# Retention in chunks of 64 inside steps of 128, in 64x64 array tiles throughout

## The chip, the core and the metric

One core of a Trainium2 chip runs the kernel. The metric is the time of one execution in microseconds of the device (us), lower is better; the median of several runs is compared. The profile is that of one execution.

## The reference

Two parts follow each other, all in float32. First a retention (attention without softmax, with a decay per head) over 8 batches, 8 heads, 576 positions and head width 64; then a gated MLP whose gate mixes positions.

```python
scores = (1/sqrt(64)) * q @ k.T                        # per batch and head
gamma  = 1 - 2.0 ** (-5 - arange(8))                   # one decay per head
ret    = scores * where(rel >= 0, gamma ** rel, 0)     # rel = row - column
x      = (ret @ v) -> [batch, 576, 512]

h      = max(x @ w_in, 0); u, v = halves of h          # w_in 512 x 1024
v_n    = (v - mean(v)) / sqrt(var(v) + 1e-6)
v_s    = einsum('ts,bsd->btd', w_spatial, v_n) + b_spatial
out    = (u * v_s) @ w_out                             # w_out 512 x 512
```

## The kernel before, in words

**The MLP.** x, the weights and the intermediates are split into a high and a low float32r part, and a product is three matmuls (`mm3`). On PE a batch goes through the stages v (x with the right half of w_in, five position blocks), u (left half, eight tiles), vs (the mixing of positions, eight tiles) and f (w_out, eight tiles). ACT and DVE take the results out of PSUM, split them and build the normalisation of v (statistics, small operations on 128x1, `vn` high and low).

**The retention** works on chunks of C = 128 positions, four per batch, and a tail of TL = 64. The two heads of a pair p lie in the two halves of the 128 partitions. For a chunk, `scores` makes k times q in 64x64 array tiles (the first key half against all 128 queries, the second against its own 64); DVE multiplies by the mask `am` and leaves `at`. `burst(b, c, nx)` issues, in this order on PE: the state update `ds` from k (scaled by POOL with `kd`) and v; the carried part, state `st` times a second copy of q (`qsc`, loaded from `q_x` and scaled by POOL with `qs`); the scores of the next chunk `nx`; and the values, `at` times v, whose second half uses array tiles of 128 rows by 64 columns. Then DVE adds the two halves of `ds` to the state, POOL multiplies the state by `sd`, and `evac` copies the result to x (ACT high part, DVE low part). Two pairs of PSUM banks alternate.

**Order.** Up to the first matmuls of batch 1's own v stage the order on every engine is that of the program: batch 0's retention goes between the splitting of w_in (`front`, `mid`, `back`) and the v blocks of batch 0, and batch 1's retention between the vs and u tiles of batch 0. From there on a scheduler orders the engines: `interleave` runs the retention of batch b+1 (a generator that yields after each burst) beside the stages of batch b. The retention's matmuls keep their program order. All DMAs are issued by SP; `load(b, c)` brings the four parts (q, k, k by position, v) of a chunk, 1 MB, two steps ahead. A recording class issues every operation, so the profile puts them all on one line, L71 (L72 after the change), and groups are told apart by the names of their tiles. In these, r is any PSUM tile of the retention, qkv a chunk's operands, at the masked scores, early, w and f are stages of splitting a weight, raw_v the right half of w_in as loaded, win and wout the split weights, pre two relu'd u tiles, s, mv and sm the statistics of v.

Of the kernel before, what the change touches and what calls it, by code (L numbers as in the profile page):

```python
# [33 lines left out]
def retention_gmlp(ctx, tc, qkv, q_x, qk_t, q_xt, v_t, w_in, w_sp, b_sp, w_out, amask, qscale, kdec, sdec, out):  # L34
# [8 lines left out]
    am = cp.tile([P, 2, NP, C], F32, name="am")  # L43
    qs = cp.tile([P, NP, C], F32, name="qs")
# [8 lines left out]
    st = [cp.tile([P, NP, D], F32, name=f"st{i}") for i in range(3)]  # L53
# [5 lines left out]
    qsc = {}  # L59
    lent = []  # L60
# [36 lines left out]
    banks = [ps_r.tile([P, 2, 512], F32, name=f"r{i}") for i in range(2)]  # L97
    for t in banks:
        ve.memset(t, 0.0)

    def pair():
        banks.reverse()
        return banks[0]
# [3 lines left out]
    def load_qsc(b, c):  # L107
        if (b, c) == (0, NC):
            t = lent[0]
        else:  # L110
            third = (b, c) == (0, 3)
            t = wk.tile([P, NP, C], F32, name=f"qsc_{b}_{c}", tag="vl" if third else "qsc", bufs=1 if third else 2)
        if c < NC:
            dma(t, q_x[b, c - 1].rearrange("p (a n) -> p a n", a=NP))
        else:
            dma(t[:, :, :TL], q_xt[b])
        qsc[b, c] = t

    def load(b, c):
        if b == 0 and c in (2, 3):  # L120
            tag = ("u", "wout0")[c - 2]
            t = cp.tile([P, NDB, S] if c == 2 else [P, NDB, DM], F32, name=f"qkv_{b}_{c}", tag=tag)
            t = t.rearrange("p a n -> p (a n)")
            if c == 2:
                lent.append(t[:, 4 * 512:].rearrange("p (a n) -> p a n", a=NP))
            t = t[:, :4 * 512].rearrange("p (a n) -> p a n", a=4)
# [17 lines left out]
        if c and (b, c) != (0, NC):  # L144
            load_qsc(b, c)
# [28 lines left out]
    dma(qs, qscale)  # L174
# [3 lines left out]
    load_qsc(0, NC)  # L178
# [61 lines left out]
    def mm(out, w, r, start, stop):  # L240
        tc.keep_in_program_order(pe.matmul(out, w, r, start=start, stop=stop))

    at = {}
    half = [slice(i * D, (i + 1) * D) for i in range(2)]

    def rows(c):
        return C if c < NC else TL

    heads = [[(p, i) for p in (2 * j, 2 * j + 1) for i in range(2)] for j in range(NP // 2)]
    heads = heads[0] + heads[1]  # L250

    def side(p, i):
# [24 lines left out]
    def burst(b, c, nx):
        n = rows(c)
        _, _, kn, vv = chunk[b, c]
        ps = pair().rearrange("p i (a n) -> p i a n", a=2)  # L280
        ds = ps[:, :, 0].rearrange("p r (a d) -> p r a d", a=NP)
        o = ps[:, :, 1].rearrange("p j (a n) -> p j a n", a=2)
        if c < NC:
            for p in range(NP):
                for r in range(2):
                    for e in (r, 1 - r):
                        h = 2 * p + side(p, e)
                        hd = slice(h * D, (h + 1) * D)
# [7 lines left out]
        for s in range(n // D):
            for p, i in heads:
                h = 2 * p + i
                e = side(p, i)
                r = half[e] if s == 0 else slice(0, n)  # L300
                t = slice(s * D, (s + 1) * D)
                mm(o[half[i], e, p // 2, t], vv[r, h * D:(h + 1) * D], at[b, c][r, i, p, t], c == 0 and s == 0 and p < 2, s == n // D - 1 and p >= 2)
        if c < NC:
            new, tmp = st[(c + 1) % 2], st[2]
            if c == 0:
                ac.copy(out=tmp, in_=ds[:, 0])
            else:
                ve.tensor_tensor(out=tmp, in0=ds[:, 0], in1=tmp, op=ALU.add)
            ve.tensor_tensor(out=new, in0=ds[:, 1], in1=tmp, op=ALU.add)
            if c + 1 < NC:  # L310
                po.tensor_tensor(out=tmp, in0=new, in1=sd.broadcast_to([P, NP, D]), op=ALU.mult)
        xo[b, c] = o[:, :, :, :n]

    def evac(b, c):
        src = xo[b, c]
        t = slice(c * C, c * C + rows(c))
        hi, lo = ((xs[b][:, i, :, t] if c < NC else xt[:, :, i]).rearrange("p (a j) n -> p j a n", j=2) for i in range(2))
        ac.copy(out=hi, in_=src)
        ve.tensor_tensor(out=lo, in0=src, in1=hi.bitcast(F32), op=ALU.subtract)
        if c == NC:  # L320
            po.tensor_copy(out=xs[b][:, :, :, t], in_=xt.rearrange("p a i n -> p i a n"))

    def retention(b):
        if b not in xs:
            xs[b] = slot(f"x_{b}")
        nxt = [(b, c) for c in range(NC + 1)] + [(b + 1, c) for c in range(2)]
        if (b, 0) not in at:
            prep(b, 0)
            scores(b, 0)
        yield 0.95  # L330
        for c in range(NC + 1):
            nx = nxt[c + 1] if nxt[c + 1][0] < B and (b, c) != (1, NC) else None
# [3 lines left out]
            evac(b, c)  # L336
# [390 lines left out]
```

## Time and profile before

| | |
|---|---|
| runs | 553.85, 554.76, 557.45 us (median 554.76) |
| profiled execution, first to last instruction | 553.7 us |
| instructions | 15312 |
| PE matmuls busy | 536.8 us (97%), 6735 instructions |
| weight loads | 498.0 us (90%) |
| DVE, ACT, POOL busy | 269.0, 207.4, 133.9 us |
| DMA | 64.08 MB |
| mean granted clock of PE | 0.988 |

No time of the profiled execution but its span is given. Busy times of matmuls overlap in parts, and their ends are modelled; starts are what to go by. A group's "idle before" is the time in which its engine stood still ahead of it, with the engine and tile that ended the wait. A chain row is a stretch of the path that ended last. A program matmul of float32 operands stands as two instructions.

### The profile page before, as it was taken

The numbers are of one execution on the slowest core, as the hardware profiler recorded it, in microseconds if no ns is written. First come the engines' busy times: TensorE is split into PE (matmuls) and PEld (weight loads), VectorE is DVE, ScalarE is ACT, GpSimd is POOL, SyncE is SP. The second block draws the span as 40 slices with busy tenths as digits, with TensorE's granted clock in tenths as the row PEclk, the third lists the DMA queues.
The fourth block names the chain that finished last, engine by engine and source line by source line (L and its number), as shares of the span: only waits on it lengthen the run. The fifth ranks groups of instructions, "written<-read, shape, count | busy, mean of one in ns | idle before, by whom it ended". The sixth has DMA issues, their size and how long they took to land.

```text
span 553.7 us, 15312 instructions
## 1 busy us (share of the span) xinstructions
PE 536.8 (97%) x6735; PEld 498.0 (90%) x6735; DVE 269.0 (49%) x588; ACT 207.4 (37%) x447; POOL 133.9 (24%) x133
## 2 busy tenths in 40 slices
PE   6897999899999999999999999999999999999997
PEld 4676998799998899989999899988999899998997
DVE  7685566922643735247351654327353373506240
ACT  4356323742223632236222551226322362226422
POOL 4747557700212111202112120121201122000000
PEclk8898899999999999999999999999999999999999
DMA  8992465002464322533225222342225342020002
GB/s 318 381 310 80 162 193 191 0 22 76 164 180 146 105 80 67 201 118 102 50 96 182 78 96 50 128 150 89 88 55 180 114 149 49 2 76 11 2 1 86
DMA packets 37045, 64.08 MB, mean 116 GB/s; under 512 B 14833, under 2 KB 27249, under 8 KB 33010
## 3 DMA queue, kind: packets, MB, share of 16 engines
q1 hardware_dynamic: 36978, 63.10, 34.5%
q8 instruction: 53, 0.87, 0.7%
q14 instruction: 14, 0.11, 0.1%
HBM read 53.65 MB, written 9.44 MB: 114 GB/s over the span
## 4 chain that ended last, share of the span: by engine, by line
PE 85%; DMA 5%; DVE 5%; ACT 3%; issue 1%; POOL 1%; SPq 0%; ACTq 0%; DVEq 0%
PE vs L71 21%; PE f L71 19%; PE u L71 17%; PE v L71 14%; PE r L71 14%; DMA qkv<-in_qkv 5%; DVE f L71 2%; DVE s L71 1%; ACT x L71 1%; DVE sm L71 1%; ACT vn L71 0%; POOL qsc L71 0%; DVE vn L71 0%; DVE w L71 0%; POOL qkv L71 0%
## 5 line engine op out<-in xcount | busy, mean ns | idle before, releaser
L71 PE MATMUL vs<-wsp,vn 128*128 128x288 f32 x768 | 115.6, 299 | 3.0 <-ACT pre L71 2.4
L71 PEld LDWEIGHTS vs<-wsp,vn 128*128 128x128 f32 x768 | 105.9, 189 | 4.9 <-ACT pre L71 2.7
L71 PE MATMUL u<-x,win 128*128 128x288 f32 x768 | 105.6, 296 | 2.2 <-ACT u L71 2.2
L71 PEld LDWEIGHTS u<-x,win 128*128 128x128 f32 x768 | 103.0, 188 | 3.7 <-POOL f L71 2.5
L71 PE MATMUL v<-win,x 128*128 128x512 f32 x384 | 93.3, 398 | 0.0
L71 PE MATMUL f<-g,wout 128*128 128x288 f32 x672 | 92.3, 296 | 0.0
L71 PEld LDWEIGHTS f<-g,wout 128*128 128x128 f32 x672 | 89.8, 188 | 0.5
L71 DVE TENSOR_TENSOR at<-r,am 128x1024 f32<-128x1024 f32 (+1 forms) x40 | 44.5, 1113 | 94.0 <-PE r L71 94.0
L71 PEld LDWEIGHTS v<-win,x 128*128 128x128 f32 x384 | 71.0, 188 | 16.6
L71 POOL TENSOR_TENSOR qsc<-qsc,qs 128x512 f32<-128x512 f32 (+1 forms) x31 | 36.1, 1165 | 177.5 <-DMA qsc<-in_q_x 112.7
L71 PEld LDWEIGHTS r<-qkv 64*64 64x64 f32 x2176 | 47.3, 139 | 14.0 <-issue 6.6
L71 PE MATMUL r<-qkv 64*64 64x64 f32 (+1 forms) x2176 | 54.0, 240 | 4.6 <-POOL qkv L71 2.8
L71 DVE BATCH_NORM_STATS2 s<-v 128x6 f32<-128x512 f32 (+1 forms) x40 | 27.7, 693 | 60.3 <-ACT v L71 59.3
L71 ACT COPY o<-f 128x288 f32<-128x288 f32 x64 | 25.6, 400 | 72.0 <-PE f L71 71.9
L71 ACT CAST g<-vs 128x288 fp32r<-128x288 f32 x56 | 22.3, 399 | 75.8 <-DVE vs L71 75.8
L71 ACT CAST x<-r 128x512 fp32r<-128x512 f32 x32 | 18.8, 586 | 60.0 <-DVE st L71 60.0
L71 POOL TENSOR_TENSOR qkv<-qkv,kd 128x512 f32<-128x512 f32 x32 | 33.3, 1043 | 32.3 <-DMA qkv<-in_qkv 25.1
L71 DVE TENSOR_TENSOR g<-vs,g 128x288 fp32r<-128x288 f32 x56 | 25.6, 458 | 26.3 <-ACT g L71 26.3
L71 PE MATMUL r<-at,qkv 64*64 64x64 f32 (+1 forms) x1152 | 37.6, 228 | 0.4 <-DVE at L71 0.4
L71 POOL TENSOR_TENSOR st<-st,sd 128x256 f32<-128x256 f32 x24 | 14.9, 620 | 93.4 <-DVE st L71 93.4
L71 DVE TENSOR_TENSOR vs<-vs,u 128x288 f32<-128x288 f32 x56 | 26.0, 464 | 23.0 <-PE vs L71 23.0
L71 PEld LDWEIGHTS r<-at,qkv 64*64 64x64 f32 (+1 forms) x1152 | 32.1, 141 | 2.8 <-DVE at L71 0.6
(73 smaller groups left out, 509.6 us busy)
## 6 DMA issues: line engine op xcount, KB each, us to landing
qkv<-in_qkv SPq DMA_DIRECT2D x31, 1024.0 KB, 5.3
out<-o SPq DMA_DIRECT2D x64, 144.0 KB, 1.8
qsc<-in_q_x SPq DMA_DIRECT2D x24, 256.0 KB, 3.2
raw_v<-in_w_in SPq DMA_DIRECT2D x4, 512.0 KB, 6.5
qkv<-in_qk_t SPq DMA_DIRECT2D x8, 256.0 KB, 3.2
qkv<-in_v_t SPq DMA_DIRECT2D x16, 128.0 KB, 3.4
raw<-in_w_in SPq DMA_DIRECT2D x4, 512.0 KB, 8.4
raw<-in_w_out SPq DMA_DIRECT2D x4, 512.0 KB, 4.1
```

The source lines that it names most:

```text
L71: ins = op(*args, **kw)
```

## The change

A step still takes 128 positions of a batch, but inside it the retention goes by two chunks of 64. Scores are only made within a chunk of 64, so all retention matmuls have 64 rows, 64 columns and a moving part of 64 columns: 272 per batch instead of 240. The state is kept at every 64 positions: `state_half` makes `sh`, the state between the two chunks, and `state_full` the state at the end (`st`); before each addition POOL makes a decayed copy of the other one (`decay`, tiles dec0 and dec1).

POOL scales q in place with `qs` (64 columns, used for both halves); the second copy of q and its loads are gone. The mask now undoes that scaling (it holds gamma to the power of minus the key's position, and zero above the diagonal) and is half as wide. So the scores read q after POOL's multiplication.

The PSUM pair `bo` holds the outputs (o, and ot for the tail), `bs` the scores and the state update; neither alternates. In `burst`, the carried part is issued in two halves, flip 1 (which reads sh for one row half of the array and st for the other) and flip 0, which exchange the row halves and banks. Between them stands `turned`, an ACT copy of two elements into an unused column of bo, which waits for the first half and which the second half waits for. The state update of the next chunk has moved from that chunk's burst into this one, behind its scores. The tail comes from one load, is scored in step 2 of a batch and finished in step 3, so there are four bursts per batch instead of five.

```diff
-    def scores(b, c):
-        n = rows(c)
-        q, k, _, _ = chunk[b, c]
-        ps = pair().rearrange("p i (a n) -> p i a n", a=NP)
-        for s in range(n // D):
-            for p, i in heads:
-                mm(ps[half[s ^ side(p, i)], i, p, s * D:n], k[half[i], p, half[s]], q[half[i], p, s * D:n], True, True)
-        a = wk.tile([P, 2, NP, C], F32, name=f"at_{b}_{c}", tag="at")
-        ve.tensor_tensor(out=a[:, :, :, :n], in0=ps[:, :, :, :n], in1=am[:, :, :, :n], op=ALU.mult)
...
+    def prep(b, c):
+        q, _, kn, _ = chunk[b, c]
+        q = q.rearrange("p a (s n) -> p a s n", s=2)
+        po.tensor_tensor(out=q, in0=q, in1=qs.rearrange("p a (s n) -> p a s n", s=1).broadcast_to([P, NP, 2, D]), op=ALU.mult)
+        kh = kn.rearrange("p (h d) -> p h d", h=H)
+        po.tensor_tensor(out=kh, in0=kh, in1=kd.broadcast_to([P, H, D]), op=ALU.mult)
...
+    def scores(b, c):
+        q, k, _, _ = chunk[b, c]
+        for p in range(NP):
+            for s in range(2):
+                for i in range(2):
+                    ts = slice(s * D, (s + 1) * D)
+                    mm(sc[half[s], i, p], k[half[i], p, ts], q[half[i], p, ts], True, True)
...
+    def carried(b, c, flip):
+        q = chunk[b, c][0]
+        for p, i in pairs:
+            s = i ^ flip
+            if c or s:
+                w = sh if s else st[c % 2]
+                mm(o[half[col(p, i)], s, p], w[half[i], p], q[half[i], p, s * D:(s + 1) * D], flip == 1 and p < 2, False)
...
+    def state_half(b, c):
+        if c == 0:
+            ac.copy(out=sh, in_=ds[:, 0])
+        else:
+            ve.tensor_tensor(out=sh, in0=ds[:, 0], in1=dec[0], op=ALU.add)
+        decay(dec[1], sh)
+
+    def state_full(b, c):
+        new = st[(c + 1) % 2]
+        ve.tensor_tensor(out=new, in0=ds[:, 1], in1=dec[1], op=ALU.add)
+        if c + 1 < NC:
+            decay(dec[0], new)
...
+    def turned():
+        ac.copy(out=bo[:1, :, 511:512], in_=warm[:1, 2:4].rearrange("p (s n) -> p s n", s=2))
+
     def burst(b, c, nx):
...
+        carried(b, c, 1)
+        turned()
         if nx:
             scores(*nx)
...
+        if c == NC - 2:
+            tail_scores(b)
+        if nx:
+            update(*nx)
+        carried(b, c, 0)
+        values(b, c)
...
-    burst(0, 0, None)
-    evac(0, 0)
-    load(0, NC)
-    fetch(0, 0)
     prep(0, 1)
     spin("idle1", 3)
-    scores(0, 1)
+    burst(0, 0, (0, 1))
+    evac(0, 0)
+    fetch(0, 0)
+    mask(0, 1)
+    state_half(0, 1)
     back(1, 2)
     mid(1, 3)
+    state_full(0, 1)
     back(1, 3, ve)
     fetch_wsp()
-    burst(0, 1, None)
     prep(0, 2)
+    burst(0, 1, (0, 2))
     evac(0, 1)
```

**What it moves in the engines' lists.** In the beginning, POOL had this list before (early is a part of w_in that POOL clamps, win1 the low part of w_in; the numbers of a tile qkv_b_c are batch and chunk):

```order
L71 TENSOR_SCALAR early_112<-early_112 128x512
L71 TENSOR_TENSOR qkv_0_0_114<-qkv_0_0_114,kd_75 128x512
L71 TENSOR_TENSOR win1_78<-early_112,win0_77 128x512 x2
L71 TENSOR_SCALAR early_112<-early_112 128x512
L71 TENSOR_TENSOR st2_88<-st1_87,sd_76 128x256
L71 TENSOR_TENSOR qkv_0_1_125<-qkv_0_1_125,kd_75 128x512
L71 TENSOR_TENSOR qsc_0_1_127<-qsc_0_1_127,qs_74 128x512
L71 TENSOR_TENSOR win1_78<-early_112,win0_77 128x512
L71 TENSOR_TENSOR st2_88<-st0_86,sd_76 128x256
L71 TENSOR_TENSOR qkv_0_2_129<-qkv_0_2_129,kd_75 128x512
```

And POOL's list after, from the second w_in clamp on:

```order
L72 TENSOR_SCALAR early_113<-early_113 128x512
L72 TENSOR_TENSOR qkv_0_1_126<-qkv_0_1_126,qs_75 128x512
L72 TENSOR_TENSOR qkv_0_1_126<-qkv_0_1_126,kd_76 128x512
L72 TENSOR_TENSOR dec1_91<-sh_89,sd_77 128x256
L72 TENSOR_TENSOR win1_79<-early_113,win0_78 128x512
L72 TENSOR_TENSOR dec0_90<-st0_87,sd_77 128x256
L72 TENSOR_TENSOR qkv_0_2_128<-qkv_0_2_128,qs_75 128x512
L72 TENSOR_TENSOR qkv_0_2_128<-qkv_0_2_128,kd_76 128x512
L72 TENSOR_TENSOR dec1_91<-sh_89,sd_77 128x256
L72 TENSOR_TENSOR dec0_90<-st1_88,sd_77 128x256
L72 TENSOR_TENSOR qkv_0_3_130<-qkv_0_3_130,qs_75 128x512
```

Each chunk's q now stands behind both decays of the chunk before. DVE at the same place after the change (x is the low part of the output, at the mask, w_13 a part of w_in):

```order
L72 TENSOR_TENSOR x_0_137<-r0_98,x_0_137 128x2x4x64
L72 TENSOR_TENSOR at_0_1_271<-r1_99,am_73 128x512
L72 TENSOR_TENSOR sh_89<-r1_99,dec0_90 128x256
L72 TENSOR_SCALAR w_13_278<-early_113 128x512
L72 SCALAR_TENSOR_TENSOR w_13_278<-raw_v_114,w_13_278 128x512 x2
L72 TENSOR_TENSOR st0_87<-r1_99,dec1_91 128x256
L72 TENSOR_TENSOR win1_79<-w_13_278,win0_78 128x512
L72 TENSOR_TENSOR x_0_137<-r0_98,x_0_137 128x2x4x64
```

Before, the mask of chunk 1 and the three w_13 operations stood ahead of the states of chunk 1 as well, but POOL's k and qsc of chunk 2 waited for nothing that came from chunk 1's values.

Second place, chunk 3 of batch 0 on ACT after the change (v_0_1 is v block 1, r0<-warm is `turned`):

```order
L72 ACTIVATE vn0_377<-v_0_0_379,sm_0_0_397 128x512
L72 ACTIVATE f_00_483<-raw_00_269 128x512
L72 ACTIVATE v_0_1_494<-v_0_1_494 128x512
L72 ACTIVATE sm_0_1_512<-mv_0_1_510,eps_94 128x1
L72 ACTIVATE v_0_1_494<-v_0_1_494,mv_0_1_510 128x512
L72 COPY r0_98<-warm_92 1x2
L72 CAST x_0_137<-r0_98 128x2x4x64
```

The copy stands behind the two operations on v block 1 that need its statistics; before, the x cast stood there and no PE instruction of the burst waited for ACT.

Third place, batch 1, step 1 on POOL after the change (f_03 is a part of w_in's left half):

```order
L72 TENSOR_TENSOR win1_79<-f_01_835,win0_78 128x4x128
L72 TENSOR_SCALAR f_03_894<-f_03_894 128x512
L72 TENSOR_TENSOR qkv_1_2_833<-qkv_1_2_833,qs_75 128x512
L72 TENSOR_TENSOR qkv_1_2_833<-qkv_1_2_833,kd_76 128x512
L72 TENSOR_TENSOR dec1_91<-sh_89,sd_77 128x256
```

Before, the same place held k and qsc of chunk 2 of batch 1, which were read one burst later; now the burst of chunk 1 reads q and k of chunk 2.

More of the change, by code (lines that the diff above doesn't have):

```diff
@@ L95, in spin @@
             pe.matmul(ps, idle[:, :P], idle, start=True, stop=True)
[L97 to L103, printed above, removed]
-    spin("idle0", 12)
[L107 to L117, printed above, removed]
+    bo, bs = (ps_r.tile([P, 2, 512], F32, name=f"r{i}") for i in range(2))
+    o = bo[:, :, :NP * D].rearrange("r s (p n) -> r s p n", p=NP)
+    ot = bo[:, :, NP * D:NP * D + 2 * TL].rearrange("r s (p n) -> r s p n", p=2)
+    sc = bs[:, :, :NP * D].rearrange("r s (p n) -> r s p n", p=NP)
+    ds = bs[:, :, NP * D:].rearrange("r s (p n) -> r s p n", p=NP)
+    spin("idle0", 12)
+    tail = {}
     def load(b, c):
@@ L143, in load, with load_tail @@
         chunk[b, c] = q, k, t[:, 2], t[:, 3]
-        if c and (b, c) != (0, NC):
-            load_qsc(b, c)
+    def load_tail(b):
+        t = ld.tile([P, 3, NP * TL], F32, name=f"tail_{b}", tag="tail", bufs=1)
+        dma(t, tails[b])
+        q, k = (t[:, i].rearrange("p (a n) -> p a n", a=NP) for i in range(2))
+        tail[b] = q, k, t[:, 2]
     staged = {}
@@ L240, in mm @@
     def mm(out, w, r, start, stop):
-        tc.keep_in_program_order(pe.matmul(out, w, r, start=start, stop=stop))
+        return tc.keep_in_program_order(pe.matmul(out, w, r, start=start, stop=stop))
     at = {}
     half = [slice(i * D, (i + 1) * D) for i in range(2)]
[L246 to L252, printed above, removed]
-        return i ^ (p % 2)
+    pairs = [(p, i) for p in range(NP) for i in range(2)]
@@ new lines, in tail_scores, with update @@
+    def tail_scores(b):
+        q, k, _ = tail[b]
+        for p in crossed:
+            for i in range(2):
+                mm(ot[half[p // 2], i, p % 2], k[half[i], p], q[half[i], p], False, False)
+    def update(b, c):
+        _, _, kn, vv = chunk[b, c]
+        for p in range(NP):
+            for s in range(2):
+                for i in range(2):
+                    hd = slice((2 * p + i) * D, (2 * p + i + 1) * D)
+                    mm(ds[half[i], s, p], kn[half[s], hd], vv[half[s], hd], True, True)
@@ new lines, in values @@
+    def values(b, c):
+        vv = chunk[b, c][3]
+        last = c == NC - 1
+        for p in range(NP):
+            for s in range(2):
+                for i in range(2):
+                    h = 2 * p + i
+                    first = c == 0 and s == 0 and p == 0
+                    mm(o[half[col(p, i)], s, p], vv[half[s], h * D:(h + 1) * D], at[b, c][half[s], i, p], first, p == NP - 1 and not last)
+        if last:
+            vv = tail[b][2]
+            for p in crossed:
+                for i in range(2):
+                    h = 2 * (p % 2) + i
+                    r = half[p // 2]
+                    mm(ot[half[col(p, i)], p // 2, p % 2], vv[r, h * D:(h + 1) * D], at[b, NC][r, i, p % 2], False, p % 2 == 1)
@@ L294, in burst @@
         if nx:
             scores(*nx)
[L296 to L311, printed above, removed]
@@ L323, in retention, with after @@
+    def after(b, c, nx):
+        if nx:
+            mask(*nx)
+        if c == NC - 2:
+            mask_tail(b)
+        evac_hi(b, c)
+        if nx:
+            state_half(*nx)
+        evac_lo(b, c)
+        if nx:
+            state_full(*nx)
+        if c == NC - 1:
+            evac_tail(b)
     def retention(b):
@@ L335, in retention @@
             burst(b, c, nx)
-            evac(b, c)
-            if nxt[c + 2:] and nxt[c + 2][0] < B and nxt[c + 2] not in chunk:
+            after(b, c, nx)
+            if nxt[c + 2][0] < B and nxt[c + 2] not in chunk:
                 load(*nxt[c + 2])
-            yield 2.65
+            if c == 0 and b not in tail:
+                load_tail(b)
+            yield 3.2
     def mm3(ps, w, r, start, stop):
@@ L509, in retention_gmlp @@
         fetch(0, i)
-    scores(0, 2)
+    mask(0, 2)
+    states(0, 2)
     vn = [cp.tile([P, NC, DH], F32R, name=f"vn{i}", tag=f"vn{i}") for i in range(2)]
@@ L521, in retention_gmlp @@
     front(0, 0)
-    scores(0, 3)
+    mask_tail(0)
+    mask(0, 3)
+    states(0, 3)
     go(v[0])
     go(v[1], 3)
-    prep(0, NC)
     burst(0, 3, None)
@@ L551, in retention_gmlp @@
     xs[1] = slot("x_1")
-    scores(1, 0)
+    group(1, 0)
+    states(1, 0)
     go(v[4])
```

168 lines of the change are left out of this document (82 added, 86 removed).

## The prediction

> **What bounds the kernel now.** I read the page first, then the chain that ended last in order of time, then the first 60 us engine by engine.
>
> ```profile
> PE 536.8 (97%) x6735; PEld 498.0 (90%) x6735; DVE 269.0 (49%) x588; ACT 207.4 (37%) x447; POOL 133.9 (24%) x133
> PEclk8898899999999999999999999999999999999999
> PE 85%; DMA 5%; DVE 5%; ACT 3%; issue 1%; POOL 1%; SPq 0%; ACTq 0%; DVEq 0%
> ```
>
> PE is the bound on average, but the 15% of the chain that is not PE, and the reduced clock, lie in the first slices. So there are two kernels to price: a steady one, from about 110 us, where each PE instruction counts and nothing else; and a beginning, where steps wait for each other. The steady one first; these are rows of the chain (start, length, engine and tile; a retention piece is "r"; from 243 the steps c=0, c=1, c=3 and the tail of one batch, then the tail without a next batch), and the row of the chunk loads:
>
> ```profile
> 243.10 2.14 PE r L71 x96
> ...
> 252.86 1.58 PE u L71 x12
> 254.44 2.58 PE r L71 x112
> 257.02 11.34 PE u L71 x84
> ...
> 282.32 2.14 PE r L71 x96
> ...
> 294.70 1.29 PE r L71 x64
> ...
> 489.98 0.62 PE r L71 x32
> ...
> 510.26 12.73 PE u L71 x96
> ...
> qkv<-in_qkv SPq DMA_DIRECT2D x31, 1024.0 KB, 5.3
> ```
>
> Each program matmul is two instructions, and four instructions of the 64x64 tiles start together; call that a round. The c=1 row has 16 instructions more than c=0, all 128 columns wide: 0.44 us for four rounds, 0.11 each. The x64 tail piece (12 rounds of 64 columns, 4 of 128) less the x32 one (8 rounds) gives (1.29-0.62-0.44)/4 = 0.058 us per 64-column round, and 0.62-8x0.058 = 0.16 us of overhead inside a piece. Outside it: u unbroken is 12.73, u broken by one piece 1.58+11.34 = 12.92, so 0.19. A purely 64x64 piece costs **0.35 us plus 0.058 per round**. The c=0 piece has 24 short and 4 long rounds, 1.83, yet takes 2.14: 0.15 more than overhead, the change into 128-row tiles for the second half of the values.
>
> **The change, steady part.** Before, a batch costs 2.14+2.58+2.58+2.14+1.29 = 10.73 and five times 0.19: 11.68 us. After, it has 272 program matmuls, 136 rounds, and about 4 more because c=0 carries into one row half only: 140x0.058 = 8.1. The order leaves five pieces in batches 3 to 6 (the third step is split by five vs matmuls): 1.75. So 9.9, a gain of 1.8 each, **-7.2**. Batch 7 has no next chunk: before 11.0, after 124 rounds and six pieces (7.2+2.1) 9.3: **-1.7**. Batch 2 is cut into ten pieces: 156 rounds and 3.5 against 13.05 (11.7, its own first scores 1.0, one more break 0.35), a gain of 0.5, and its scores of chunk 2 come only 29 vs matmuls (3.9 us) after the load could be issued, while the page has 5.3 us from issue to landing and the q multiplication follows; I take a wait of 2: **+1.5**. Steady sum **-7.4**. Inside a piece the small ACT copy stands between the two carried halves; 16 rounds (0.93 us) cover it. In the steady batches the cover for load, q and k (5.3+1.3+1.0) is the 11.8 us of other matmuls between steps. If either is gone, PE waits by the difference.
>
> **The beginning.** These are the groups that the new steps consist of (mean ns behind the busy time):
>
> ```profile
> L71 POOL TENSOR_TENSOR qkv<-qkv,kd 128x512 f32<-128x512 f32 x32 | 33.3, 1043 | 32.3 <-DMA qkv<-in_qkv 25.1 <-PE vs L71 4.3 <-issue 1.9
> L71 POOL TENSOR_TENSOR qsc<-qsc,qs 128x512 f32<-128x512 f32 x24 | 31.0, 1290 | 129.2 <-DMA qsc<-in_q_x 112.7 <-PE vs L71 13.0 <-PE f L71 3.5
> L71 DVE TENSOR_TENSOR st<-r,st 128x256 f32<-128x256 f32 x56 | 23.6, 421 | 4.3 <-PE r L71 2.7 <-ACT st L71 0.6
> L71 DVE TENSOR_TENSOR x<-r,x 128x512 fp32r<-128x512 f32 x32 | 22.1, 691 | 19.3 <-ACT x L71 19.3
> L71 ACT CAST x<-r 128x512 fp32r<-128x512 f32 x32 | 18.8, 586 | 60.0 <-DVE st L71 60.0
> L71 POOL TENSOR_TENSOR st<-st,sd 128x256 f32<-128x256 f32 x24 | 14.9, 620 | 93.4 <-DVE st L71 93.4
> L71 DVE TENSOR_TENSOR at<-r,am 128x512 f32<-128x512 f32 x8 | 5.5, 690 | 3.6 <-PE r L71 3.6
> L71 POOL TENSOR_TENSOR win<-early,win 128x512 fp32r<-128x512 f32 x3 | 3.9, 1294 | 0.5 <-ACT early L71 0.5
> ```
>
> And where the beginning stands now:
>
> ```profile
> 7.39 1.49 POOL L71 TENSOR_SCALAR early<-early 128x512 f32<-128x512 f32 x1 [5.51 <-ACT early L71]
> 10.50 1.04 POOL L71 TENSOR_TENSOR qkv<-qkv,kd 128x512 f32<-128x512 f32 x1 [1.62 <-DMA qkv<-in_qkv]
> 16.07 2.34 PE L71 MATMUL r<-qkv 64*64 64x128 f32 x64 [0.29 <-DMA qkv<-in_qkv]
> 18.86 0.68 DVE L71 TENSOR_SCALAR w<-early 128x512 int32<-128x512 int32 x1
> 19.57 1.42 DVE L71 SCALAR_TENSOR_TENSOR w<-raw_v,w 128x512 int32<-128x512 int32 x2
> 20.92 0.90 PE L71 MATMUL r<-qkv 64*64 64x128 f32 x32
> 21.75 3.07 PE L71 MATMUL v<-win,x 128*128 128x512 f32 x12
> 31.89 0.74 DVE L71 SCALAR_TENSOR_TENSOR vn<-v,sm,vn 128x512 fp32r<-128x512 f32 x1
> 32.74 0.70 DVE L71 BATCH_NORM_STATS2 s<-v 128x6 f32<-128x512 f32 x1
> 33.90 0.64 ACT L71 ACTIVATE v<-v,mv 128x512 f32<-128x512 f32 x1
> 44.41 3.45 PE L71 MATMUL u<-x,win 128*128 128x288 f32 x24
> 50.28 1.46 PE L71 MATMUL vs<-wsp,vn 128*128 128x288 f32 x9 [2.42 <-ACT pre L71]
> 64.99 0.85 PE L71 MATMUL r<-qkv 64*64 64x128 f32 x32
> 66.39 1.48 POOL L71 TENSOR_SCALAR f<-f 128x512 f32<-128x512 f32 x1
> ```
>
> Now the scores need only a DMA (16.07; 20.92 without a wait). After, they read q that POOL has scaled, and POOL works its list in order. For chunk 1: early until 8.88, q of chunk 0 to 10.2, k (its data landed at 10.5, some 0.3 sooner as the mask is halved) to 11.25, win 1.29, two decays 0.62 with DVE's state between them, to 14.6, win to 15.9, the second early to 17.4, q 1.29: the scores of chunk 1 start at **18.7**, not 16.07.
>
> From one q to the next stands a closed loop, as the lists of the four engines give it: q 1.29, k 1.04, update 0.47, carried 0.24, values of the chunk before 0.47, ACT x 0.59, DVE x 0.69, mask 0.69, state half 0.42, POOL decay 0.62, DVE state 0.42, POOL decay 0.62, and only then the next q. That is 7.6, and 0.6 for a dozen hand-overs (estimated at 0.05 each): **8.2 us per chunk**. Before, the scores of chunks 1 and 2 were 4.85 apart.
> - Chunk 1 to 2: DVE has win's three operations (0.69+1.42) between state half and state, which hide one decay: 8.2+1.5, so q of chunk 2 starts at 17.4+9.7 = 27.1, and v block 0 follows its scores, update, carried and values at about 30.5 instead of 21.75.
> - Chunk 2 to 3: q of chunk 3 at 35.3 (v block 0 is hidden in it).
> - Chunk 3: q, k, the tail's q (half of 1.29, 0.73 with its start), rounds 1.2, ACT x, DVE x, v block 0's four small ones 0.85, two masks 1.1, state half: 43.8. POOL takes one more early-type operation (1.5) ahead of the decay, DVE state: 45.8. The ACT copy between the carried halves now stands behind ACT's work on v block 1, which waits for DVE's vn and statistics: 0.74+0.70+0.18, ACT 0.29+0.64, copy 0.25 (unseen; nearest ACT rows 0.2 to 0.4): carried goes on at 49.0, values done 50.1.
> - Then PE has v 2, 3 and 4 (7.5), scores and update of batch 1 (1.3): u starts at 58.9 instead of 44.4: **+14.5**. With q at 1.04 and no hand-overs it is +11.
>
> Second, the clock. Busy times of the engines in stretches of the trace's clock periods (PE, PEld, DVE, ACT, POOL, then the granted clock):
>
> ```profile
> 7.48:10.89 3.41, 0.90 (x32) 0.79 (x32) 3.30 (x5) 1.07 (x2) 1.79 (x2) 1.00 1.03 412
> 10.89:14.30 3.41, 2.71 (x65) 2.47 (x66) 3.23 (x5) 2.28 (x5) 2.86 (x3) 0.50 1.06 427
> 14.30:17.72 3.42, 3.04 (x36) 2.04 (x36) 1.88 (x5) 1.89 (x4) 3.36 (x4) 0.50 1.01 414
> 103.05:106.46 3.41, 2.16 (x15) 1.84 (x13) 3.41 (x11) 2.19 (x6) 3.38 (x3) 1.00 0.00 0
> ```
>
> A stretch in which PE worked 0.90 of 3.41 us was followed by two at half clock; one with 2.16 was not. After the change PE stands still for 3 to 5 us four times before 50 us (14.2 to 18.7, 25 to 28, 33 to 35, 44 to 49), so most of its work to 55 us falls into halved stretches. Some 10 us of PE work is on the chain there; half of that again: **+5**, with 0 and +8 as ends.
>
> The Trainium skill's page "TensorE: Matmul & The Clock Gate" (section "What's actually happening") has a window of 3.4 us, after an idle one half clock, after one busy one full clock again. One halved window per still one, not two as in these rows, would make this term about +2.5 and the forecast 2.5 lower. The trace has two, and I go by it.
>
> Third, before the first vs (2.42 us of waiting now) DVE has the state of batch 1 ahead of v's statistics, and it waits for a decay behind POOL's wsp work: **+2** (0 to 3). Fourth, batch 1, step 1: the scores ran at 64.99 without waiting. After, they need q behind the POOL operation that ends at 67.87: 69.2, update a k later at 70.2, 4.5 late; step 2, whose load follows step 1, waits for q and k after landing; half clock again after such a stop. +6, less 2 that batch 1's rounds gain: **+4** (1 to 8). Fewer bytes (q_x and the doubled mask are gone) bring chunks about 1 to 3 us sooner, but POOL's list decides when they are used, so nothing.
>
> **Sum**, against the profiled span of 553.7: 553.7 - 7.4 + 14.5 + 5 + 2 + 4 = 571.8. The median shown, 554.76, stands 1.1 above that span: **573**.
>
> **Rivals.** (1) *Faster: PE is the bound throughout.* If the loop costs the first 60 us no more than PE's present stops there can swallow, the steady -7.4 decides: 547. For it: PE 97% busy. Against: the loop is 8.2 long where PE has 1.2 us of rounds and a v block of 2.8 per chunk. It decides once the beginning loses under 7.4. Chance 0.07. (2) *No difference:* the loop is real but short (q at 1.04, no half clock, batch 1 gains): +11 +0 +0 -3 -7.4 gives 554 to 560. Chance 0.09. (3) *The rounds do not run four abreast* where consecutive scores share a column half: 36 rounds a batch would take twice 0.058, 8x2.1 = +17: 590. Against it: the rounds now go through other tile orders in scores, update and values at the same 0.058. Chance 0.04. (4) *More half clock than counted,* batch 1's stops included: 580 to 586. Chance 0.10. The forecast keeps 0.70.
>
> **How the numbers follow.** Low end: +11, no clock, no third term, +1: 559 with the offset. High end: 14.5+8+3+8 and a steady gain of 5 only: 583. About 1% is what a measurement of this kernel can tell from no change, so the bounds are 549 and 560. Faster 0.07; same 0.11 (rival 2 and the low edge); slower 0.82.
>
> **What would show it.** In the profile after: r matmuls of 64x64 alone, 4352 of them, steady batches about 63.3 us long instead of 65.1; the first v matmul near 30 to 33 us; POOL's q operations at 17 and 27 us, each followed by PE's scores; PEclk low in the second to fifth slices; the chain with more POOL and DVE. I am wrong if v block 0 starts before 25 us (the loop is then not closed as I read the lists), if the steady batch does not shrink (then a round is not 0.058), or if PE's carried halves wait for the ACT copy in every step.

## The result, and the profile after

The changed kernel takes 580.72 us (578.85 to 582.28) against 554.48 for the kernel before: a ratio of 1.0459, with an interval of 1.0425 to 1.0493. The forecast was 573, in a range of 559 to 583. The profiled execution has a span of 577.1 (553.7 before), so the traces show 23.4 of the 26.2 us. A trace is one execution, and executions of one kernel lie up to 7.4 us apart here (573.58 to 580.94 us in the first experiment), so a late position in a trace says less than a median.

These lines of the page stand against the three shown first of the kernel before (engines, granted clock by slice, the chain that ended last):

```profile
PE 532.2 (92%) x7247; PEld 493.9 (86%) x7247; DVE 244.8 (42%) x586; ACT 210.7 (37%) x479; POOL 163.0 (28%) x173
PEclk8577887999999999999999999999999999999999
PE 78%; POOL 8%; DVE 5%; DMA 3%; issue 2%; ACT 2%; SPq 0%; ACTq 0%; POOLq 0%; DVEq 0%
```

PE has less work in all (532.2 for 536.8) and holds less of the chain; POOL went from 1% of it to 8%. The reduced clock still lies in the first slices, only lower. Where each stage starts on PE says where the time goes:

| start of | before | after | difference |
|---|---|---|---|
| v block 0 of batch 0 | 21.75 | 33.36 | +11.6 |
| u of batch 0 | 44.41 | 66.77 | +22.4 |
| vs of batch 0 | 50.28 | 73.53 | +23.3 |
| f of batch 0 | 118.81 | 147.71 | +28.9 |
| v of batch 2 | 172.24 | 203.03 | +30.8 |
| v of batch 3 | 237.34 | 266.68 | +29.3 |
| last matmul | 550.30 | 573.56 | +23.3 |

**The steady batches.** The chain, with one batch from its u piece to the next one's:

```profile
286.78 2.02 PE r L72 x128
...
302.39 1.56 PE r L72 x96
...
316.21 2.49 PE r L72 x160
...
335.65 1.96 PE r L72 x107
...
349.99 2.02 PE r L72 x128
```

The period is 349.99-286.78 = 63.2 us, where the forecast had 63.3 and the kernel before 65.1 (from batch 2's v stage to batch 3's in the table). The five pieces take 8.89 us, and 0.19 more each by the break: 9.84. The groups of r matmuls by tile (behind the count stand the shortest, median and longest in ns, then the first and last start), the first and the last of seven, whose counts make 4352:

```profile
L72 PE MATMUL r<-qkv x2048: 218/218/366, 10.7 to 494.1; 64*64 64x64 f32 x187
...
L72 PE MATMUL r<-att,tail x128: 218/218/311, 53.7 to 511.7; 64*64 64x64 f32 x128
```

All are 64x64 with 64 columns. Two stops of about 0.25 and 1.1 us in the seventh batch's retention (430 and 445 us) have no cause that the profile shows; this is the longer one's row:

```profile
446.56 1.61 PE L72 MATMUL f<-g,wout 128*128 128x288 f32 x11 [0.97 <-issue]
```

**The beginning.** Waits of PE up to 140 us (total, times, longest), before and then after:

```profile
PE r L71 <- POOL qkv L71: 2.8, 1, 2.8
```

```profile
PE r L72 <- POOL qkv L72: 23.1, 8, 4.8
```

And the rows of the timeline on which the three laps of the loop, the copy between the carried halves and the entry into batch 1 can be read (dec is a decay):

```profile
18.75 1.26 POOL L72 TENSOR_TENSOR qkv<-qkv,qs 128x512 f32<-128x512 f32 x1
...
25.90 0.61 POOL L72 TENSOR_TENSOR dec<-sh,sd 128x256 f32<-128x256 f32 x1 [4.89 <-DVE sh L72]
...
28.29 0.61 POOL L72 TENSOR_TENSOR dec<-st,sd 128x256 f32<-128x256 f32 x1 [0.53 <-DVE st L72]
28.86 1.26 POOL L72 TENSOR_TENSOR qkv<-qkv,qs 128x512 f32<-128x512 f32 x1
...
37.60 1.26 POOL L72 TENSOR_TENSOR qkv<-qkv,qs 128x512 f32<-128x512 f32 x1
```

```profile
20.07 2.13 PE L72 MATMUL r<-qkv 64*64 64x64 f32 x64 [4.03 <-POOL qkv L72]
...
30.17 2.13 PE L72 MATMUL r<-qkv 64*64 64x64 f32 x64 [3.59 <-POOL qkv L72]
...
38.92 0.69 PE L72 MATMUL r<-qkv 64*64 64x64 f32 x32 [2.11 <-POOL qkv L72]
...
52.12 0.36 PE L72 MATMUL r<-qkv,st 64*64 64x64 f32 x1 [2.08 <-ACT r L72]
...
64.55 0.69 PE L72 MATMUL r<-qkv 64*64 64x64 f32 x32 [1.35 <-POOL qkv L72]
66.14 0.69 PE L72 MATMUL r<-qkv 64*64 64x64 f32 x32 [0.91 <-DVE at L72]
```

PE starts each chunk's scores when POOL has done that chunk's q, 10.1 and 8.7 us apart, as the forecast's closed loop has it (9.7 and 8.2). Each q after the first stands behind both decays of the chunk before, and PE's list has no other work to put into the gap.

### The profile page after: what moved, and what is told of

Read it like the earlier page. It is cut to its first block, busy times and chain, and to the rows that moved or that the text cites. A ratio compares the mean times of both kernels' runs of the same rounds, so it can differ in the third digit from the quotient of the medians.

```text
span 577.1 us, 16334 instructions
## 1 busy us (share of the span) xinstructions
PE 532.2 (92%) x7247; PEld 493.9 (86%) x7247; DVE 244.8 (42%) x586; ACT 210.7 (37%) x479; POOL 163.0 (28%) x173
## 4 chain that ended last, share of the span: by engine, by line
PE 78%; POOL 8%; DVE 5%; DMA 3%; issue 2%; ACT 2%; SPq 0%; ACTq 0%; POOLq 0%; DVEq 0%
PE vs L72 19%; PE f L72 18%; PE u L72 15%; PE v L72 14%; PE r L72 13%; POOL qkv L72 4%; DVE f L72 2%; DMA qkv<-in_qkv 2%; DMA raw_v<-in_w_in 1%; POOL f L72 1%; POOL dec L72 1%; ACT x L72 1%; DVE x L72 1%; DVE st L72 1%; POOL win L72 1%
## 5 line engine op out<-in xcount | busy, mean ns | idle before, releaser
L72 PE MATMUL vs<-wsp,vn 128*128 128x288 f32 x768 | 117.8, 300 | 1.8 <-ACT pre L72 1.8
L72 PE MATMUL u<-x,win 128*128 128x288 f32 x768 | 107.0, 299 | 2.5 <-ACT u L72 2.4
L72 PEld LDWEIGHTS u<-x,win 128*128 128x128 f32 x768 | 104.5, 191 | 4.0 <-ACT u L72 2.7
L72 POOL TENSOR_TENSOR dec<-sh,sd 128x256 f32<-128x256 f32 x32 | 19.6, 613 | 220.4 <-DVE sh L72 163.6
L72 PE MATMUL r<-qkv 64*64 64x64 f32 x2048 | 43.6, 233 | 26.2 <-POOL qkv L72 25.1
L72 PEld LDWEIGHTS r<-qkv 64*64 64x64 f32 x2048 | 38.2, 146 | 29.8 <-POOL qkv L72 28.8
L72 POOL TENSOR_TENSOR qkv<-qkv,qs 128x512 f32<-128x512 f32 x32 | 41.0, 1282 | 51.7 <-DMA qkv<-in_qkv 42.4
L72 ACT CAST g<-vs 128x288 fp32r<-128x288 f32 x56 | 22.4, 400 | 75.0 <-DVE vs L72 75.0
L72 DVE TENSOR_TENSOR at<-r,am 128x512 f32<-128x512 f32 x32 | 22.0, 688 | 59.9 <-PE r L72 59.8
L72 ACT CAST x<-r 128x512 fp32r<-128x512 f32 x32 | 18.7, 586 | 69.4 <-PE r L72 39.9
L72 ACT ACTIVATE u<-u 128x288 f32<-128x288 f32 x56 | 22.8, 407 | 38.5 <-PE u L72 38.3
L72 DVE TENSOR_TENSOR x<-r,x 128x512 fp32r<-128x512 f32 x32 | 21.9, 685 | 31.5 <-ACT x L72 31.5
```

The costliest lines, as they stand in the source:

```text
L72: ins = op(*args, **kw)
```

## The experiments

Each is compared with runs of the kernel before on the same chip (medians of 554.3 to 555.1). Theory A throughout: the beginning is lost to the order of POOL's, ACT's and DVE's lists, not to the new arithmetic. Up to v block 0, traces of kernels with the same lists agree to 0.1 us (33.36, 33.32 and 33.44 in the changed kernel and in the second and third experiment).

### 1. q of batch 0 ahead of the decays

```diff
     states(0, 0)
+    prep(0, 1)
     back(1, 1)
     front(1, 3)
     mid(1, 2)
-    prep(0, 1)
+    prep(0, 2)
...
     fetch_wsp()
-    prep(0, 2)
+    prep(0, 3)
...
     go(v[0], 3)
-    prep(0, 3)
     prep_tail(0)
```

> The changed kernel with POOL's scaling of q and k for chunks 1, 2 and 3 of batch 0 issued ahead of the decays that it stood behind; nothing else is moved. Theory A (the order on POOL closes the loop: q of the next chunk waits for both decays): scores of chunk 1 start near 17.4 instead of 20.07 us, scores of chunks 2 and 3 no longer wait for POOL, a chunk takes about 5.5 instead of 8.7 to 10.1 us, the first v matmul comes near 27 instead of 33.4 us, u near 58 instead of 66.8, and the time falls by about 8 (5 to 11) from 580.7 to near 573. Rival B (the loop is closed by ACT's and DVE's copies, mask and states, and q only comes last by chance): only the 2.7 us of chunk 1 are gained, 577 to 579.

Measured: 578.25 us, 1.0405 (1.035 to 1.046), in time not told apart from the changed kernel. In the trace v block 0 starts at 29.04 and u at 59.85 (A: 27 and 58), 6.9 us sooner than in the changed kernel. Behind the wait for q the next wait appears:

```profile
25.84 1.99 PE L72 MATMUL r<-qkv 64*64 64x64 f32 x64 [1.68 <-DVE st L72]
```

The scores of chunk 2, whose q is ready, now wait for DVE's state, which reads the same PSUM bank. So A holds for the first 7 us, and B for what is behind them. The end of the trace came only 5.3 sooner, since from batch 1's vs stage to batch 2's v stage it took 43.8 us instead of 41.9; and the traced run took 573.58, while the median, 2.5 below the changed kernel's, is where B had it.

### 2. q of batch 1 ahead of the weight work

```diff
     states(0, 3)
+    prep(1, 0)
...
     load_tail(1)
-    prep(1, 0)
...
     front(0, 2)
+    prep(1, 2)
     vs_tile(0, 2)
...
     go(ret)
+    prep_tail(1)
+    prep(1, 3)
     vs_tile(1, 0)
```

A `prep` that has been done is not done again where it stood before.

> The changed kernel with the scaling of q and k for chunks 0, 2, 3 and the tail of batch 1 issued ahead of POOL's splitting of weights; nothing else is moved. Theory A (PE's three stops before scores of batch 1, 1.5+1.1 at 62.8, 4.9 at 85.4 and 2.3 at 100.1 us, are POOL's list and nothing more): about 7 us of these go, and 574 is left. Rival B (the weight splits that now stand 2.3 us later on POOL are late for u, so the stops move to the u tiles): a gain under 3, 578 to 581.

Measured: 572.62 us, 1.0286 (1.0238 to 1.0335). Waits of PE from 60 to 140 us in the changed kernel, then here:

```profile
PE r L72 <- POOL qkv L72: 8.3, 3, 4.8
```

```profile
PE vs L72 <- ACT pre L72: 3.6, 1, 3.6
...
PE r L72 <- POOL qkv L72: 1.4, 3, 0.8
```

A is right: 6.9 us of waiting for POOL went, 1.8 of it into the wait for ACT ahead of vs (1.8 before). The f stage of batch 0 starts 8.9 sooner, and between the same two stages as above it took 45.7 us, 3.8 more than in the changed kernel.

### 3. Two places at chunk 3

```diff
-    front(0, 0)
     mask_tail(0)
     mask(0, 3)
     states(0, 3)
+    front(0, 0)
     go(v[0])
-    go(v[1], 3)
+    go(v[1], 2)
     burst(0, 3, None)
+    go(v[1])
```

> The changed kernel with two moves at chunk 3 of batch 0: POOL's clamp of the first left-half weight part goes behind the decay, and ACT's work on the statistics of v block 1 goes behind the small copy between the carried halves. Theory A (PE's stops at 47.3 to 49.7 and 49.8 to 52.1 us are these two list places): the second carried half starts near 48.6 instead of 52.1, all behind it is 3.5 earlier, near 577. Rival B (the weight part is then late for u, or batch 1's q, which POOL has at 63.2 behind its wsp work, is the bound anyway): under 1 us, 580.

```profile
48.66 0.27 PE L72 MATMUL r<-qkv,st 64*64 64x64 f32 x1 [0.27 <-ACT r L72]
```

The second carried half starts at 48.66, as A has it to a tenth (52.12 before the edit), and u 3.7 sooner. But the time is 578.78, 1.0426 (1.0399 to 1.0454), not told apart: the f stage of batch 0 is only 2.1 sooner, and between the two stages it took 45.3. A is right at the place; the time lies between A's 577 and B's 580.

### 4 and 8. Fill the stops of PE to hold the clock

```diff
+    def hold(n):
+        for i in range(n):
+            pe.matmul(bs[:, 0, :256], idle[:, :P], idle[:, :256], start=True, stop=True)
...
         carried(b, c, 1)
         turned()
+        if b == 0:
+            hold((16, 13, 8, 8)[c])
```

The first fill is 21 instead of 12 matmuls, and batch 1's first scores have 6 ahead of them.

> The changed kernel with matmuls of no use (zeros into the score bank, some 3 us each) in six of PE's stops before 65 us; no wait is removed. Theory A (the forecast's clock term: PE's work on the chain between 10 and 62 us runs at half clock because of the stops): the granted clock stays at or near 1.0 up to 65 us, the pieces of 3.4 us in the chain at 20.1 and 30.2 us shrink to about 2.2, v blocks 2 to 4 from 8.9 to 7.6, and the time falls by 4 to 6, to about 576. Rival B (the stops are set by POOL, and what PE gains it waits again): the clock rises, the time stays within 1.5 of 580.7. Rival C (fill is longer than the stop): slower.

Measured: 580.2 us, 1.0455 (1.0408 to 1.0501), the time that B had. But the fill was too short ahead of chunk 1, and the clock still fell to 0.5 three times, so A had no fair trial. The eighth run has more of it ((30, 36, 14, 18), and in four further stops):

> The changed kernel with matmuls of no use in all of PE's stops of over 1 us before 65 us, about twice as many as in the fourth experiment, whose fill covered only half of each stop and whose clock still fell to 0.5 three times; the lists of the other engines are as in the changed kernel. Theory A (the clock is a cost of its own): granted clock near 1.0 up to 62 us, v blocks 2 to 4 take 7.6 instead of 8.9, u starts 4 to 5 us before 66.8, near 576. Rival B (POOL's list sets the start whatever PE's clock is): clock near 1.0, u at most 1.5 sooner, 579 to 581. Rival C (fill outlasts the stops): slower.

Measured: 585.34 us, 1.0548 (1.0513 to 1.0583). Stretches of the clock's length (PE, PEld, DVE, ACT, POOL busy, granted clock), three of the changed kernel and the same three of the eighth:

```profile
17.72:21.13 3.41, 1.06 (x36) 1.01 (x37) 0.49 (x1) 0.00 (x0) 3.29 (x3) 0.50 0.99 394
21.13:24.55 3.42, 2.35 (x76) 2.16 (x72) 0.35 (x1) 0.97 (x3) 0.00 (x0) 0.50 0.46 165
27.96:31.37 3.41, 1.20 (x40) 1.14 (x44) 0.94 (x2) 0.58 (x2) 2.83 (x3) 0.50 0.70 224
```

```profile
17.72:21.13 3.41, 2.33 (x67) 1.99 (x69) 0.11 (x1) 0.00 (x0) 2.96 (x3) 1.00 1.00 405
21.13:24.55 3.42, 3.29 (x73) 2.50 (x64) 1.69 (x4) 1.57 (x3) 0.00 (x0) 1.00 0.43 152
27.96:31.37 3.41, 3.41 (x30) 3.33 (x28) 0.00 (x0) 0.00 (x0) 1.86 (x2) 1.00 0.96 341
```

The clock is full, yet v block 0 starts at 33.22 for 33.36. POOL's q of chunk 2 and what PE does then say why:

```profile
27.52 1.29 POOL L72 TENSOR_TENSOR qkv<-qkv,qs 128x512 f32<-128x512 f32 x1
```

```profile
27.74 3.75 PE L72 MATMUL r<-wsp 128*128 128x256 f32 x30
31.42 1.16 PE L72 MATMUL r<-qkv 64*64 64x64 f32 x64
```

q came 1.3 us sooner than at half clock (27.52 for 28.86), and the fill outlasted the stop by more than that (scores at 31.42, q done at 28.8): rival C, and again in chunk 3, where v block 2 starts at 55.98 for 54.25. So neither run prices the clock well. What they show: 1.3 us at chunk 2's q, and in the fourth run 1.3 at v block 1 (42.06 for 43.37), of which 0.5 is left at u (66.27), since batch 1's scores wait for POOL's q all the same (64.05 for 64.55). The twelfth run tries the fill with the lists cleared.

### 5. The three list edits together

> The edits of the first three experiments together (q of batch 0 ahead of the decays, the tail's q too; q of batch 1 ahead of the weight work; the two moves at chunk 3). Theory A (each removes waits of its own place): their gains add up at the start of batch 0's f stage, which came 6.7, 8.9 and 2.1 us sooner than in the changed kernel, so it starts near 130 us instead of 147.7; batch 2 hands 4 of it back as it did in the three runs; 567. Rival B (behind each wait stands the next, state by DVE and POOL): the f stage starts at 135 to 138, 571 to 575.

Measured: 562.48 us, 1.0136 (1.0092 to 1.018): 18 us of the 26 that the change had cost, with no arithmetic changed. The f stage starts at 133.02, 14.7 sooner where the single gains add up to 17.7: between A and B. The time is under either's, since between the two stages nothing was handed back (39.9 us; 39.8 in the kernel before).

### 6 and 7. The state ahead of the weight work; loads in halves

```diff
     back(1, 1)
-    front(1, 3)
     mid(1, 2)
...
     burst(0, 0, (0, 1))
-    evac(0, 0)
+    after(0, 0, (0, 1))
     fetch(0, 0)
-    mask(0, 1)
-    state_half(0, 1)
+    front(1, 3)
     back(1, 2)
     mid(1, 3)
-    state_full(0, 1)
     back(1, 3, ve)
```

The two bursts behind it get `after` in the same way.

> As the one before, and in batch 0 DVE does the mask and the half state ahead of x's low part, the state ahead of the weight parts, and POOL clamps the last right-half weight part behind both decays. Theory A (once q is early, scores of the next chunk wait for DVE's state: 23.85 to 25.84 us in the first experiment): scores of chunk 2 start 2 us sooner, v block 0 near 27 us, u near 52, and the time is 3 to 4 below that of the three edits, about 563. Rival B (win's low part for v block 0 is now what comes last): v block 0 not before 29, less than 1 us gained.

Measured: 568.62 us, 1.0245 (1.0197 to 1.0294), 6 slower than without. Scores of chunk 2 start 2.2 us sooner, as A has it (23.60 for 25.84), but ACT's list shows a mechanism that neither theory had:

```profile
27.91 0.59 ACT L72 CAST win<-w 128x512 fp32r<-128x512 f32 x1 [4.20 <-DVE w L72]
28.39 0.15 ACT L72 COPY r<-warm 1x2 f32<-1x2 f32 x1
```

The small copy stands behind a weight cast that waits for DVE, whose weight work is now later, so PE waits 3.0 us for it (its second carried half starts at 28.59): v block 0 at 30.08 instead of 29.04. And between the two stages it took 47.5 us. There the chain that ended last runs through a load (start, length):

```profile
168.42 6.98 DMA qkv<-in_qkv
...
175.53 1.27 POOL qkv L72
...
176.85 3.52 PE r L72 x126
```

The seventh run loads each chunk in two DMAs, q and k first:

```diff
+        elif b:
+            dma(t[:, :2], qkv[b, c, :, :2])
+            dma(t[:, 2:], qkv[b, c, :, 2:])
         else:
             dma(t, qkv[b, c])
```

> As the one before, and from batch 1 on a chunk is loaded by two DMAs, q and k first. Theory A (what batch 2 hands back, 2 to 6 us between the start of its vs stage of batch 1 and its own v stage, is landing of 5 us plus POOL's q behind a load that can't be issued sooner): q lands about 1.5 us sooner per step, the stops of 2 us in batch 2 go, 3 to 4 us less than without. Rival B (the place of the pieces decides it, which the scheduler gives): within 1.5 us of the one before.

Measured: 566.79 us, 1.0206 (1.0167 to 1.0245), not told apart from the sixth in time; the stretch is 44.5, shorter by 3.0. PE's waits from 140 to 200 us in the sixth, then in the seventh:

```profile
PE r L72 <- POOL qkv L72: 5.1, 2, 3.0
```

```profile
PE r L72 <- POOL qkv L72: 3.2, 3, 1.5
```

The time fell by 1.8 (A had 3 to 4, B at most 1.5) and 1.9 us of waiting went: the loads are part of it.

### 9 and 10. The copy's and the masks' waits; three buffers

```diff
         scores(b, c)
-        mask(b, c)
         update(b, c)
+        mask(b, c)
...
     burst(0, 1, (0, 2))
+    mid(1, 3)
+    back(1, 3, ve)
...
-    go(v[0], 3)
+    go(v[0], 2)
     burst(0, 2, (0, 3))
...
-    states(1, 0)
+    state_half(1, 0)
     go(v[4])
```

The tenth has in addition:

```diff
-            t = ld.tile([P, 4, 512], F32, name=f"qkv_{b}_{c}", tag="qkv")
+            t = ld.tile([P, 4, 512], F32, name=f"qkv_{b}_{c}", tag="qkv", bufs=3)
...
     load_tail(0)
+    load(1, 0)
...
-                load(*nxt[c + 2])
+                load(*nxt[c + 3])
```

> The three edits of the fifth experiment, and the waits that its trace shows behind them: the small copy of chunk 2 ahead of v block 0's statistics on ACT (PE stood 1.8 at 33.2 us before the tail's scores), the one of chunk 1 no longer behind the weight casts that made it 3.3 late in the sixth experiment, DVE's state of chunk 1 ahead of the weight work, the first updates of batches 0 and 1 ahead of the mask they waited for (1.1 and 2.8 us), and in batch 1 the full state behind v's statistics and the relu of the first u tile ahead of the last weight casts (3.8 us before vs). Theory A (each of these waits is on the path): u near 49 instead of 55.7, vs near 53, batch 0's f stage near 125, 554 to 556. Rival B (ACT and DVE work of v blocks 3 and 4, which no edit moves, sets vs): vs not before 58, 558 to 560. Rival C (batch 2's place of pieces changes again, as in the sixth experiment): the start is earlier and 3 to 6 us of it are handed back there.

> As the one before, with three buffers for the chunks instead of two, so that each load is issued one step sooner. Theory A (batch 2's steps close a loop of load, landing 5 us, POOL's q and k and the burst that frees the buffer, 8 to 10 us long where batch 1's vs and f stages leave 8.5 per step): no stop of PE before scores in batches 1 and 2, the stretch from batch 1's vs to batch 2's v falls from 40 to 47 us to about 39, and the time is 3 to 6 below the one before, under 552, faster than the kernel before. Rival B (the pieces' places cost it, not the loads): within 1.5 of the one before.

Measured: 559.96 us, 1.0092 (1.0059 to 1.0124), and 556.2, 1.0017 (0.9989 to 1.0045). In the ninth, u starts at 50.58 and the f stage of batch 0 at 126.33, near A's 49 and 125, but the traced run took 555.46; the median is where B had it, though vs does not come as late as B said (55.76). In the tenth, PE has one stop of any size listed from 137 to 200 us, and it isn't one for q:

```profile
PE f L72 <- issue: 0.3, 1, 0.3
```

The stretch takes 38.5 us, as A has it, though the time missed A's 552 and is not told apart from the kernel before; B's 1.5 fell too, at 3.8 below the ninth. In the traces the stretch took 39.6 to 47.5 us in the ten kernels with two buffers and 38.0 to 38.5 in the three with three, and the waits in it are for q, with the load ahead of it in the sixth's chain: so the loop of load, POOL's q and the burst that frees the buffer is what costs there. Its cost does not follow from how early the stretch is entered. The fourth and eighth run entered it later than the changed kernel and still took 44.2 and 46.5, the fifth and ninth entered it 14.7 and 20.9 sooner and took 39.9 and 39.6. One trace of each does not tell what sets it.

### 11 and 12. Bulk loads later; the clock again

```diff
-    front(1, 3)
     mid(1, 2)
-    prep(0, 2)
+    prep_q(0, 2)
...
     state_full(0, 1)
+    front(1, 3)
...
-    load(1, 1)
-    for i in range(1, NDB):
-        fetch(0, i)
...
+    load_tail(1)
+    load(1, 1)
+    for i in range(1, NDB):
+        fetch(0, i)
     load(1, 2)
     fetch(2, 0)
-    load_tail(1)
```

> As the three-buffer kernel, with three moves: POOL does q of chunk 2 and both decays ahead of the last right-half clamp; the 2.5 MB of loads that ran from 31 to 40 us (the other left-half weight parts, two chunks) are issued behind the tail's load, which waits for chunk 3 of batch 0; ACT's high part of v block 3 goes ahead of the second u relu. Theory A (PE's stop of 3.3 us in v block 1 at 34 us, with nothing that the profile shows, is its program's code arriving late behind that bulk; it was 1.8 to 3.3 in every kernel that reached this place while the bulk ran, and 0 in the changed kernel that came there later): the stop goes to under 1, scores of chunk 2 start 1.8 sooner, u near 47 to 48, the end 4 to 6 sooner: 550 to 552, faster than the kernel before by 0.5 to 1%. Rival B (the stop is not due to the bulk): the stop stays at 2 to 3.5, gain under 3: 553 to 555. Rival C (the late loads are themselves waited for in batch 1): 556 or more.

The twelfth adds to it:

```diff
-    spin("idle0", 12)
+    spin("idle0", 31)
...
         turned()
+        if (b, c) == (0, 0):
+            hold(20)
...
+    spin("idle2", 5)
     burst(0, 1, (0, 2))
```

> As the one before, with PE filled with matmuls of no use up to its first scores (19 more of 512 columns), ahead of chunk 1's scores (20 of 256) and ahead of chunk 1's burst (5 of 512). Theory A (the clock has a price only where POOL's list no longer covers it; here the granted clock was 0.5 in 10.9 to 14.3, 17.7 to 21.1 and 24.5 to 28 us): r pieces up to v block 0 take half, v block 0 starts 1 to 2 us sooner, 1 to 2 off the time. Rival B (the stretch up to chunk 1's scores waits for its landing and behind it for the states on DVE and POOL): under 0.5 us.

Measured: 554.39 us, 0.9988 (0.9977 to 0.9999), and 551.88, 0.9949 (0.9935 to 0.9963). The stop in v block 1, in the tenth and then in the eleventh, each with the DMA queue for instructions in the one microsecond in which it moved a packet (35 to 36, 33 to 34):

```profile
37.78 1.71 PE L72 MATMUL v<-win,x 128*128 128x512 f32 x5 [3.30 <-issue]
```

```profile
q8 instruction: 1, 0.02, 6.6%
```

```profile
36.37 1.79 PE L72 MATMUL v<-win,x 128*128 128x512 f32 x7 [0.41 <-issue]
```

```profile
q8 instruction: 1, 0.02, 7.4%
```

With the bulk moved, the stop shrinks from 3.3 to 0.4, as A said of the place. But half of that is no gain: the stop ends only 1.4 us sooner (36.37 for 37.78), and PE reaches the place 1.5 us later (35.96 for 34.48), because v block 0, though it starts 3.0 sooner, now waits for weight parts and the steps behind it for DVE. That PE's instructions came late is consistent with the packets, not shown. And vs now waits 1.9 for the last weight part on POOL. The time is in B's range, and not told apart from the tenth.

The twelfth is faster than the kernel before, by 0.5%. The same stretches as above:

```profile
17.72:21.13 3.41, 3.20 (x111) 2.67 (x109) 1.57 (x4) 0.93 (x2) 3.41 (x4) 1.00 1.02 418
21.13:24.55 3.42, 2.59 (x116) 1.99 (x115) 0.81 (x2) 1.21 (x4) 3.42 (x5) 1.00 1.00 397
27.96:31.37 3.41, 1.63 (x39) 0.93 (x42) 2.62 (x6) 0.80 (x3) 1.88 (x4) 1.00 0.94 285
```

The clock stays at 1.00 up to 38 us. The time falls by 2.5 us, but v block 0 starts no sooner: 25.42 (25.30 without the fill). That is B's number, yet not B's reason. Scores of chunk 2 start 1.3 us sooner (half a microsecond of it from a load that landed earlier), and then PE stands in the values of chunk 1. The scores in the eleventh run, then the same place in the twelfth:

```profile
23.51 1.16 PE L72 MATMUL r<-qkv 64*64 64x64 f32 x64
```

```profile
22.22 1.24 PE L72 MATMUL r<-qkv 64*64 64x64 f32 x64 [0.19 <-DVE st L72]
23.51 0.51 PE L72 MATMUL r<-at,qkv 64*64 64x64 f32 x18
25.03 0.45 PE L72 MATMUL r<-at,qkv 64*64 64x64 f32 x14 [1.01 <-issue]
```

The stop of 1.01 has no releaser, like those in v block 1, where this kernel has none, and a packet on the instruction queue moved from 22 to 23 us. So what A had came and was lost again; u starts at 49.94 (51.49), and the gain in time lies behind v block 0. What part of these 2.5 us is clock and what is code or POOL's list in another phase, the runs don't tell apart. The kernel before was not run with such a fill, so whether the 0.5% is the change's is not shown.

## Why the prediction was right, point by point

- **Steady rounds: right.** Five pieces took 9.84 us per batch with their breaks (forecast 9.9); the period fell by 1.9 (forecast 1.8). From the f stage of batch 0 to the end 5.6 were gained instead of 7.4; 1.4 of the difference are the two stops at 430 and 445 us.
- **Batch 2: right in mechanism.** With waits for q of 2.1 (forecast 2), the stretch was 2.1 longer (forecast 1.5). The sixth run's chain and the tenth run show the loop. That it could cost up to 7.7 us, by kernel (47.5 in the sixth for 39.8), was not seen.
- **The loop on POOL: right, and the decisive term, but mis-sized.** u came 22.4 later, where the forecast had 14.5 for the lists and 5 for the clock, nearly all of it ahead of u. The hand-overs, which had no row in the prediction, show as 0.05 to 0.06 (q done at 20.01, 30.12 and 38.86, scores at 20.07, 30.17 and 38.92). Its laps were 0.4 and 0.5 too short, the first scores 1.4 too early (20.07 for 18.7), the last carried half 0.8 too quick; the waits of 2.3 for batch 1's q and mask at 64.55 and 66.14, where POOL's list has x, two wsp parts and win ahead of q, were not in the sum at all, though the list showed it.
- **The clock: the term that failed.** It fell as forecast: 0.50 in all stretches from 10.9 to 31.4. But the price of 5 was added to a sum of lists, and the lists cover much of it: full clock brought chunk 2's q 1.3 sooner, and filling the stops moved v block 1 by 1.3 and u by 0.5. With one fill too short and the other too long, these are signs of a small price and no measurement of it. Nor do the prediction's rows make a threshold: there a stretch with 2.16 us of PE work was followed by full clock, in the twelfth run one with 2.14 (34.78 to 38.20) by 0.58. On the clock's return the Trainium skill's page "TensorE: Matmul & The Clock Gate" (section "What's actually happening") asks for one busy window; in the changed kernel a stretch with 2.35 of 3.42 us busy (21.13 to 24.55) was followed by another at 0.50, so that was not busy enough here.
- **The third and fourth terms.** From u to vs 0.9 was lost (forecast 2), from vs to batch 0's f stage 5.6 (forecast 4); in the second run the same way took 6.7 less by POOL's order alone, so this was POOL's list again.
- **The wait for the small copy** was forecast for chunk 3 alone (carried on at 49.0; measured 52.12). It is a hazard in any step where ACT's list has a wait ahead of it, as the sixth run shows.
- **The rivals.** PE bound throughout fell with u at 66.77. That rounds would not run four abreast fell with the 63.2 us period. That there is more half clock than counted ended at the right time (580 to 586) by another way: the fifth run took 18 us away by the lists alone, while the fourth and eighth, with more clock, took nothing.

The total was nearer than its parts, and that is luck: with the fourth run's 0.5 for the clock, the lists' term was some 7 short, the clock's some 4 too high, and the steady gain 1.8 too high. That the change makes the kernel slower, and by the loop on POOL, was not luck.

## What to carry to other kernels

A scaling that is moved from a copy onto the operand itself puts an in-order engine ahead of the first matmul that reads it; follow what stands in front of it in that engine's list, in the first steps above all, where no other work hides it. A gain per steady step is worth its count of steps only if the beginning is rearranged with it: here the same arithmetic was 4.6% slower or level with the kernel before (0.9988) by the order of the lists, the loads and one buffer, and 0.5% faster with fill. Even in that kernel batch 0's f stage starts 6.4 us later than before (125.17 for 118.81); what gains is the batches behind it. Don't add a clock's price to a sum of waits: first ask what else arrives at that time.

## What was not expected of the hardware

- Scores of the next chunk waited for DVE's reading of the state update in the same PSUM bank, though not of the same columns (1.68 us in the first experiment). Whether the chip asks for that or the program's semaphores do, the runs don't show.
- In v block 1 PE stopped with nothing to wait for in the profile, for 1.5 to 3.3 us in the six kernels that got there before 40 us with the bulk loads where they were (experiments 1, 5, 6, 7, 9 and 10), and the stop ended 2.4 to 2.6 us after the start of a packet on the instruction queue. Loads alone don't do it: the kernel before has no such stop, though 312 to 339 GB/s moved from 21 to 38 us.
- Fill has its price: in the eighth run it outlasted the stop before chunk 2's scores by 2.6 us and took back all that the full clock had brought there.
